# Two-layer FNet and attention kernel: single-row start, identity transposes, fused Newton steps, halved last copies

## The chip, the cores and the metric

One NeuronCore of a Trainium2 chip runs the kernel; the other cores are idle. The metric is the device time of one execution in microseconds (us). TensorE (PE in the profile, PEld for its weight loads) multiplies, VectorE (DVE), ScalarE (ACT) and GpSimd (POOL) compute elementwise, and SyncE (SP) issues most DMAs.

## What is computed

The input `x` is 2048 x 512, float32. Two layers run one after the other, each with the same weights:

```python
x = x + fnet(layernorm(x))       # Real(DFT_seq(DFT_hidden(.))): Cr @ (x @ Dr.T) - Ci @ (x @ Di.T)
x = x + attention(layernorm(x))  # 32 heads of 16; one k and one v shared by all heads; softmax; @ wo
...
def _layernorm(x, axis=-1, eps=1e-5):
    m = jnp.mean(x, axis=axis, keepdims=True)
    v = jnp.var(x, axis=axis, keepdims=True)
    return (x - m) / jnp.sqrt(v + eps)
```

## The kernel before

The sequence is cut into 16 row tiles of 128 (`NT`). Large products are made from two parts of each operand in a reduced format: a high part (`xnh`, `ch`) and the rest (`xnl`, `cl`). `mm3` (L86) issues three matmuls for one product: high by high, high by low, low by high. The low part is what is left after the high part is subtracted.

The order of work is written out by hand: every engine takes its instructions in the order of the code, and semaphores hold an instruction until what it needs is there. In phase A of a layer, `phase_a` loops over 128 steps `n`. In step `n` the matrix row tile `n % 16` of the sequence DFT is multiplied with the normalized row tile of the same number, into four accumulators `z`. The first 16 steps of layer 0 are those in which the rows are normalized, one after the other, two steps ahead of TensorE.

What the first steps do on each engine:

- `ld` and `c_load` issue the loads on SyncE: rows singly (256 KB), matrix tiles in pairs (`craw`, 512 KB, three buffers).
- `ln_stats` (L143, L144) takes mean and variance of a row on VectorE. `ln_root` (L149) takes the square root on ScalarE, for two rows, and adds `eps` to the variance on GpSimd (L150). `ln_inv` takes the reciprocal on VectorE (L156), then refines it by one Newton step, four small instructions on GpSimd (L157 to L160), or on VectorE where it is told so.
- `ln_app` normalizes a row in place on VectorE (L191). `ln_split` casts it to `xnh` on ScalarE (L658) and subtracts to get `xnl` on GpSimd (L659).
- `c_split` casts `craw` to `ch` on ScalarE (L78) and subtracts to get `cl` on VectorE (L79).
- `ln_step(n)` orders these: split row `n + 2`; in even steps the inverse of rows `n + 4` and `n + 5`; normalize row `n + 3`; in even steps the statistics of rows `n + 6` and `n + 7` and their root. In steps 4, 6, 8 and 10 `qd_zero` issues two DMAs from GpSimd (L121) behind that.

`a_start` writes out what comes before step 0: rows 0 and 1 are normalized together by `ln_rstd`, each operation an instruction of its own on VectorE.

Phase A also makes keys, values, queries and the maxima of the scores. Its last rows 14 and 15 are normalized singly, with `ln_inv` on VectorE, and transposed by `tr` (L268). Phase B is the attention: scores (L980), exponential (L983), product with the values (L994). `pv` copies a finished accumulator in two halves into one tile (L997 on ScalarE, L998 on VectorE). `finish` handles the last half tile of the last layer: four transposes of the copy (L1065), products with `wo` for the first half of the heads (`o_mm(0)`, `o_mm(1)`), scaling (L1070, L1073), two transposes (L1079), the split into high and low, the last products, and `o_add`, which adds to `x` (L1056) and issues the store on SyncE (L1057).

Of the kernel before, what the change touches and what calls it, by code (L numbers as in the profile page):

```python
# [17 lines left out]
P = 128  # L18
# [4 lines left out]
NT = S // P  # L23
# [16 lines left out]
]  # L40
ROWS = 48
KEPT = [e for e in EARLY if e[0]]
QSLOT = (8, 0, 1, "h", "l", 8, 0, 1, "h", "l", 8, 0, 1, 8, 0, 1)
HALF = NPAIR // 2
# [3 lines left out]
def fnet_mqa_kernel(ctx: ExitStack, tc: tile.TileContext, x_in, ct, dt_, wq, wkv, wo, out):  # L48
# [12 lines left out]
    def half(k, dtype=F32):  # L61
        return sb.tile([P, D], dtype, name=f"row{k}")
# [23 lines left out]
    def mm3(ps_, ah, al, bh, bl, start, stop):  # L86
        nc.tensor.matmul(ps_, ah, bh, start=start, stop=False)  # L87
        nc.tensor.matmul(ps_, ah, bl, start=False, stop=False)  # L88
        nc.tensor.matmul(ps_, al, bh, start=False, stop=stop)  # L89
# [51 lines left out]
    def ln_stats(x, t):  # L141
        st = sb.tile([P, 2, 6], F32, name="bst", bufs=2)
        nc.vector.bn_stats(st[:, 0, :], x)  # L143
        nc.vector.bn_aggr(mv[:, t, :], st[:, 0, :])  # L144

    def ln_root(t0, n):
        v = sb.tile([P, 4], F32, name="lnv", bufs=2)[:, :n]
        w = sb.tile([P, 4], F32, name="lnw", bufs=2)[:, :n]
        nc.scalar.activation(w, mv[:, t0:t0 + n, 1], AF.Sqrt, bias=eps)  # L149
        nc.gpsimd.tensor_scalar(v, mv[:, t0:t0 + n, 1], EPS, None, op0=ALU.add)  # L150
        return t0, n, v, w

    def ln_inv(t0, n, v, w, eng=None):
        r = rs[:, t0:t0 + n]
        e = eng or nc.gpsimd
        nc.vector.reciprocal(r, w)  # L156
        e.tensor_mul(w, r, r)  # L157
        e.tensor_mul(w, w, v)
        e.tensor_scalar(w, w, -0.5, 1.5, op0=ALU.mult, op1=ALU.add)
        e.tensor_mul(r, r, w)  # L160
# [35 lines left out]
    def make_layer(L, src, mid, dst, last):  # L196
# [11 lines left out]
        def c_load(n):  # L208
            if n < 128 and n % 2 == 0:
                tb, c, s = where(n)  # L210
                r = raws[n // 2] = raw_tile()
                if n < 112:
                    nc.sync.dma_start(r, ct[c, tb, s // 2])
                else:
                    h, sp = divmod(n - 112, 8)
                    for j in range(2):
                        nc.sync.dma_start(r[:, j, :].rearrange("p (a t) -> p a t", a=2),
                                          ct[c, tb, sp + j][:, :, 256 * h:256 * h + 256])

        def c_split(n):  # L220
            if n < 128:
# [386 lines left out]
        def a_start():  # L608
            if L:
                c_load(0)  # L610
                c_load(2)
            if L == 0:
                xs = {}

                def ld(t):
                    xs[t] = half(t % 8)
                    nc.sync.dma_start(xs[t], src[t])

                ld(0)
                ld(1)  # L620
                c_load(0)
                ld(2)
                ld(3)
                c_load(2)
                ld(4)
                ld(5)
                c_load(4)
                ld(6)
                ld(7)
                st["xs"], st["ld"] = xs, ld  # L630
                ln_stats(xs[0], 0)
                ln_stats(xs[1], 1)
                ln_rstd(0, 2)
                ln_app(0)
                ln_split(0)
                c_split(0)
                ln_app(1)
                ln_split(1)
                for t in (2, 3):
                    ln_stats(xs[t], t)  # L640
                r = ln_root(2, 2)
                c_split(1)
                for t in (4, 5):
                    ln_stats(xs[t], t)
                ln_inv(*r)
                st["root"] = ln_root(4, 2)
                ln_app(2)
            else:
                c_load(4)
                c_split(0)  # L650
                c_split(1)

        def ln_app(t):
            ln_apply(st["xs"][t], st["xs"][t], t)

        def ln_split(t):
            x = st["xs"][t]
            nc.scalar.copy(xnh[:, t, :], x)  # L658
            nc.gpsimd.tensor_sub(xnl[:, t, :], x, f(xnh[:, t, :]))  # L659

        def ln_step(n):
            if n + 2 < NT:
                ln_split(n + 2)
            if n % 2 == 0 and n + 4 < NT:
                ln_inv(*st["root"])
            if n % 2 == 0 and n + 8 < NT:
                st["ld"](n + 8)
                st["ld"](n + 9)
            if n + 3 < NT:
                ln_app(n + 3)  # L670
            if n % 2 == 0 and n + 6 < NT:
# [61 lines left out]
        def phase_a(extra):  # L733
# [120 lines left out]
            for n in range(128):  # L854
# [32 lines left out]
                                      lambda d: z_split_half(z[4 * h:4 * h + 4], h, d))  # L887
                for d in range(NK):
                    dsl = slice(d * P, (d + 1) * P)
                    if n < ROWS:  # L890
# [96 lines left out]
        def pv(i, s_):  # L987
            hf, c = divmod(s_, NT)
            if c == 0:
                acc[i, hf] = bank("z")  # L990
            a = acc[i, hf]
            pt = ptiles.pop((i, s_))
            for j in range(4):
                nc.tensor.matmul(a[32 * j:32 * j + 32, :], v1[:, c, :], pt[:, j, :], start=c == 0, stop=c == NT - 1)  # L994
            if c == NT - 1:
                oa = half(hf)
                nc.scalar.copy(oa[:, :256], a[:, :256])  # L997
                nc.vector.tensor_copy(oa[:, 256:], a[:, 256:])  # L998
                acc[i, hf] = oa

        bt = {}

# [38 lines left out]
            nc.gpsimd.tensor_copy(bt["oh"][:, cs], bt["ot"][:, cs])  # L1041
            nc.gpsimd.tensor_sub(bt["ol"][:, cs], bt["ot"][:, cs], f(bt["oh"][:, cs]))

        def o_mm(k):
            if k == 0:
                bt["po"] = bank("y")
            ks = slice(k * P, (k + 1) * P)
            mm3(bt["po"], bt["oh"][:, ks], bt["ol"][:, ks], woh[:, k, :], wol[:, k, :], k == 0, k == NK - 1)

        def o_proj(i):  # L1050
# [2 lines left out]
            o_add(i)  # L1053

        def o_add(i):
            nc.vector.tensor_add(bt["x"], bt["po"], bt["x"])  # L1056
            (nc.sync if last else nc.gpsimd).dma_start(dst[i], bt["x"])  # L1057

        def finish():
            i = NT - 1  # L1060
            oa = acc.pop((i, 1))
            x_load(i)
            pt = bank("y")
            for b in range(4):
                nc.tensor.transpose(pt[:, b * P:(b + 1) * P], oa[:, b * P:(b + 1) * P], ident)  # L1065
# [12 lines left out]
            for jj in range(2):  # L1078
                nc.tensor.transpose(pt[:, jj * P:(jj + 1) * P], on[:, jj * P:(jj + 1) * P], ident)  # L1079
# [176 lines left out]
```

## Time and profile before

| what | value |
|---|---|
| median of 3 runs | 3546.07 us (3544.29 to 3546.45) |
| profiled execution | 3549.72 us, span 3547.9 us |
| granted TensorE clock, mean | 0.995 |
| busy share of the span | PE 99%, DVE 77%, ACT 71%, POOL 23% |
| TensorE, 0 to 20 us | 10.11 us busy |
| TensorE, 20 to 40 us | 19.33 us busy |
| TensorE, 40 to 61.5 us | 20.47 us busy |

A row of a timeline gives the start in us, the duration in us, the engine, the line, the operation, what it writes and reads, the shapes, and in brackets the idle time of the engine before it with what ended it. A row of the waits gives the sum in us, the times and the longest. The difference between the profiled execution's time and its span lies around the program and is not touched by the change.

### The profile page before, as it was taken

Reading aid. Unit: us, or ns where it says so; the run is one execution under the profiler, and the core shown is the slowest. Engines: PE = TensorE matmul, PEld = TensorE weight load, DVE = VectorE, ACT = ScalarE, POOL = GpSimd, SP = SyncE. Lnnn points to the kernel's source line nnn. Section 1 sums busy time; section 2 is a strip of 40 time slices with the busy share of each in tenths; the row PEclk is TensorE's granted clock in tenths of the full one; section 3 lists DMA queues with packets and bytes.
Section 4 is the critical chain, followed back from the end, with each engine's and each line's share of the span. In section 5 each row is a group of like instructions: output and inputs, shape, how many; then the busy total and the mean of one; then the engine's idle time right before and its main releaser. Section 6 shows DMA issues by size and latency. Waiting matters only on the chain.

```text
span 3547.9 us, 64282 instructions
## 1 busy us (share of the span) xinstructions
PE 3505.9 (99%) x24576; PEld 1874.8 (53%) x24576; DVE 2714.7 (77%) x4892; ACT 2503.3 (71%) x3210; POOL 830.5 (23%) x1262
## 2 busy tenths in 40 slices
PE   8999999999999999999999999999999999999999
PEld 6887878433333333333378878883333333333333
DVE  6267776888888888888432777768888888888883
ACT  4223733888888888888932247438888888888888
POOL 4244342211221122112213443422101110111011
PEclk9999999999999999999999999999999999999999
DMA  6435252311111100111144342523111111011100
GB/s 191 150 144 167 80 165 87 85 56 34 35 35 51 36 23 23 49 34 26 40 137 128 127 150 90 153 66 88 47 37 35 49 34 38 23 35 37 37 23 25
DMA packets 224900, 254.55 MB, mean 72 GB/s; under 512 B 52880, under 2 KB 174800, under 8 KB 217424
## 3 DMA queue, kind: packets, MB, share of 16 engines
q1 hardware_dynamic: 210384, 233.12, 21.6%
q0 software_dynamic: 14208, 17.33, 1.6%
q8 instruction: 193, 3.16, 0.4%
q14 instruction: 115, 0.94, 0.1%
HBM read 187.16 MB, written 65.27 MB: 71 GB/s over the span
## 4 chain that ended last, share of the span: by engine, by line
PE 91%; issue 2%; DVE 2%; ACT 2%; POOL 1%; DMA 1%; SPq 0%; ACTq 0%; POOLq 0%; DVEq 0%
PE z L994 29%; PE x L980 19%; PE y L408 13%; PE x L809 11%; PE y L87 3%; PE y L88 3%; PE y L89 2%; PE y L475 2%; PE x L87 2%; PE x L89 2%; PE x L88 2%; PE x L593 1%; PE z L475 1%; DVE row L191 1%; POOL cl L79 1%
## 5 line engine op out<-in xcount | busy, mean ns | idle before, releaser
L983 ACT ACTIVATE slot<-x 128x1024 f32<-128x1024 f32 x2000 | 1945.9, 1024 | 284.5 <-PE x L980 276.2
L409 DVE TENSOR_REDUCE mxp<-y 128x1 f32<-128x512 f32 x2944 | 1849.6, 684 | 181.5 <-PE y L408 168.7
L994 PE MATMUL z<-slot,v 128*32 128x512 f32 x8192 | 1096.3, 605 | 1.6 <-DVE lnv L1105 0.7
L980 PE MATMUL x<-slot,kz 64*128 64x512 f32 x2976 | 677.3, 450 | 2.2 <-DMA slot<-craw 1.7
L980 PEld LDWEIGHTS x<-slot,kz 64*128 64x128 f32 x2976 | 279.2, 184 | 744.7 <-ACT slot L983 685.8
L408 PE MATMUL y<-kz,slot 64*128 64x512 f32 x2176 | 581.6, 397 | 1.9 <-DVE mxp L409 1.9
L809 PE MATMUL x<-cl,xnh 64*128 64x512 f32 (+1 forms) x1536 | 355.8, 357 | 0.0
L994 PEld LDWEIGHTS z<-slot,v 128*32 128x32 f32 x8192 | 163.4, 108 | 363.7 <-issue 332.8
L809 PE MATMUL x<-ch,xnh 64*128 64x512 f32 (+1 forms) x1536 | 348.1, 361 | 2.3 <-ACT row L796 2.2
L809 PE MATMUL x<-ch,xnl 64*128 64x512 f32 (+1 forms) x1536 | 346.2, 362 | 0.9 <-ACT xnl L580 0.9
L408 PEld LDWEIGHTS y<-kz,slot 64*128 64x128 f32 x2176 | 276.7, 186 | 22.8 <-DVE mxp L409 10.8
L79 POOL TENSOR_TENSOR cl<-craw,ch 128x512 fp32r<-128x512 f32 x176 | 223.9, 1295 | 225.5 <-ACT ch L78 174.3
L78 ACT CAST ch<-craw 128x512 fp32r<-128x512 f32 x256 | 154.6, 622 | 170.9 <-PE x L89 87.1
L475 PE MATMUL y<-kz,slot 64*128 64x512 f32 x690 | 271.7, 405 | 2.1 <-ACT rel L479 1.2
L543 POOL DMA_DIRECT2D slot<-mt x224 | 112.1, 508 | 585.2 <-PE y L408 490.1
L809 PEld LDWEIGHTS x<-ch,xnh 64*128 64x128 f32 x1536 | 213.1, 188 | 23.3 <-issue 5.2
L809 PEld LDWEIGHTS x<-cl,xnh 64*128 64x128 f32 x1536 | 217.7, 188 | 12.6
L489 DVE TENSOR_REDUCE mxe<-y 128x1 f32<-128x512 f32 x316 | 198.8, 679 | 29.3 <-PE y L475 28.7
L809 PEld LDWEIGHTS x<-ch,xnl 64*128 64x128 f32 x1536 | 209.7, 187 | 21.1 <-issue 5.9
L1035 POOL TENSOR_TENSOR row<-row,row 128x256 f32<-128x256 f32 x63 | 46.5, 738 | 700.3 <-DMA row<-rd 654.0
L87 PE MATMUL x<-ch,xnh 128*128 128x512 f32 x384 | 154.3, 402 | 9.1 <-ACT ch L78 8.4
L89 PE MATMUL x<-ch,xnl 128*128 128x512 f32 x384 | 153.4, 399 | 2.6 <-POOL xnl L659 2.6
(198 smaller groups left out, 4143.3 us busy)
## 6 DMA issues: line engine op xcount, KB each, us to landing
craw<-ct_in SPq DMA_DIRECT2D x112, 512.0 KB
slot<-qd SPq DMA_DIRECT2D x44, 1024.0 KB
qd<-row SPq DMA_DIRECT2D x144, 128.0 KB
od<-row SPq DMA_DIRECT2D x252, 64.0 KB
row<-wqd SPq DMA_DIRECT2D x48, 256.0 KB
row<-x_in SPq DMA_DIRECT2D x32, 256.0 KB
mid<-row POOLq DMA_DIRECT2D x32, 256.0 KB, 2.4
craw<-ct_in SPq DMA_DIRECT2D x32, 256.0 KB
```

Source lines behind the costliest of these rows:

```text
L79: (eng or nc.vector).tensor_sub(lo, raw, f(hi))
L87: nc.tensor.matmul(ps_, ah, bh, start=start, stop=False)
L88: nc.tensor.matmul(ps_, ah, bl, start=False, stop=False)
L89: nc.tensor.matmul(ps_, al, bh, start=False, stop=stop)
L408: nc.tensor.matmul(pm, o.qT[i][gs, pr, :], kz[gs, c0:c0 + n], start=True, stop=True)
L409: nc.vector.reduce_max(to, pm, axis=AX.X)
L475: nc.tensor.matmul(pm, o.qT[i][gs, pr, :], k[gs, c0:c0 + 512], start=True, stop=True)
L489: nc.vector.reduce_max(to, pm, axis=AX.X)
L809: nc.tensor.matmul(z[d], a[gs, s, d * P:(d + 1) * P], b[gs, :], start=first and q < 2 and e == 0, stop=last and q > 1 and e == len(turns) - 1)
L980: nc.tensor.matmul(st["e"][:, g, :], kz[64 * g:64 * g + KR, c * P:(c + 1) * P], o.qT[i][64 * g:64 * g + KR, cp:cp + 4, :], start=True, sto ...
L983: nc.scalar.activation(ptiles[i, s_][:, 2 * w:2 * w + 2, :], st.pop("e"), AF.Exp, scale=DH ** -0.5)
L994: nc.tensor.matmul(a[32 * j:32 * j + 32, :], v1[:, c, :], pt[:, j, :], start=c == 0, stop=c == NT - 1)
```

## The change

Six edits, at both ends of the kernel:

- Eleven transposes of the identity (`WARM`) are issued on TensorE ahead of the first matmul, into a buffer that nothing reads.
- Rows 0 and 1 are normalized one at a time (`first`): the normalized row is written straight to `xnh` by VectorE (a second L191-like instruction normalizes the row in place for `xnl`), and the matrix tile is split by `c_hi` and `c_lo`. The order of the instructions up to step 0 is changed with it. `c_split` skips tiles that are split already.
- The first matrix tile is loaded in two halves, each behind a row.
- In steps 0 and 1 of layer 0 TensorE does four matmuls of each kind (high by high, high by low, low by high) in turn, in place of three for each accumulator.
- `ln_inv` with an engine given uses three fused instructions (`scalar_tensor_tensor`); `ln_step` now gives it VectorE. Without an engine it does the former steps on GpSimd, and the addition of `eps` moves to it from `ln_root`.
- At the end, the second half of the last accumulator is copied to a tile of its own; one of the matmuls of `o_mm(1)` is moved behind the last transposes; the last addition and store are done in halves, the second store issued by ScalarE.

```diff
+WARM = 11
...
     def ln_root(t0, n):
-        v = sb.tile([P, 4], F32, name="lnv", bufs=2)[:, :n]
         w = sb.tile([P, 4], F32, name="lnw", bufs=2)[:, :n]
         nc.scalar.activation(w, mv[:, t0:t0 + n, 1], AF.Sqrt, bias=eps)
-        nc.gpsimd.tensor_scalar(v, mv[:, t0:t0 + n, 1], EPS, None, op0=ALU.add)
-        return t0, n, v, w
-
-    def ln_inv(t0, n, v, w, eng=None):
+        return t0, n, w
+
+    def ln_inv(t0, n, w, eng=None):
         r = rs[:, t0:t0 + n]
-        e = eng or nc.gpsimd
         nc.vector.reciprocal(r, w)
+        if eng:
+            eng.scalar_tensor_tensor(w, r, -0.5, r, op0=ALU.mult, op1=ALU.mult)
+            eng.scalar_tensor_tensor(w, mv[:, t0:t0 + n, 1], EPS, w, op0=ALU.add, op1=ALU.mult)
+            eng.scalar_tensor_tensor(r, w, 1.5, r, op0=ALU.add, op1=ALU.mult)
+            return
+        v = sb.tile([P, 4], F32, name="lnv", bufs=2)[:, :n]
+        e = nc.gpsimd
+        e.tensor_scalar(v, mv[:, t0:t0 + n, 1], EPS, None, op0=ALU.add)
...
+                def c_row(j):
+                    nc.sync.dma_start(raws[0][:, j, :], ct[0, 0, 0][:, j, :])
+
+                def c_hi(n):
+                    hls[n] = hl_tiles()
+                    nc.scalar.copy(hls[n][0], raws[n // 2][:, n % 2, :])
+
+                def c_lo(n):
+                    nc.vector.tensor_sub(hls[n][1], raws[n // 2][:, n % 2, :], f(hls[n][0]))
+
+                def first(t, r):
+                    ln_inv(*r, nc.vector)
+                    ln_apply(xnh[:, t, :], xs[t], t)
+                    c_lo(t)
+                    ln_app(t)
+                    nc.gpsimd.tensor_sub(xnl[:, t, :], xs[t], f(xnh[:, t, :]))
+
                 ld(0)
+                c_load(0)
+                c_row(0)
                 ld(1)
-                c_load(0)
+                c_row(1)
...
+                warm = bank("y")
+                for k in range(WARM):
+                    nc.tensor.transpose(warm[:, P * (k % 4):P * (k % 4) + P], ident, ident)
                 ln_stats(xs[0], 0)
+                r = ln_root(0, 1)
+                c_hi(0)
+                c_hi(1)
+                first(0, r)
                 ln_stats(xs[1], 1)
-                ln_rstd(0, 2)
-                ln_app(0)
-                ln_split(0)
-                c_split(0)
-                ln_app(1)
-                ln_split(1)
-                for t in (2, 3):
-                    ln_stats(xs[t], t)
+                r = ln_root(1, 1)
+                ln_stats(xs[2], 2)
+                first(1, r)
+                ln_stats(xs[3], 3)
                 r = ln_root(2, 2)
-                c_split(1)
+                c_hi(2)
+                c_lo(2)
+                ln_inv(*r, nc.vector)
+                ln_app(2)
                 for t in (4, 5):
                     ln_stats(xs[t], t)
-                ln_inv(*r)
                 st["root"] = ln_root(4, 2)
-                ln_app(2)
...
             if n % 2 == 0 and n + 4 < NT:
-                ln_inv(*st["root"])
+                ln_inv(*st["root"], nc.vector)
...
+                    if n < 2 and L == 0:
+                        for e in range(NK) if d < 3 else ():
+                            a, b = ((xnh, ch), (xnh, cl), (xnl, ch))[d]
+                            nc.tensor.matmul(z[e], a[:, s, e * P:(e + 1) * P], b, start=(n, d) == (0, 0), stop=False)
...
+                ob = half(0)[:, 256:] if last and (i, hf) == (NT - 1, 1) else oa[:, 256:]
                 nc.scalar.copy(oa[:, :256], a[:, :256])
-                nc.vector.tensor_copy(oa[:, 256:], a[:, 256:])
+                nc.vector.tensor_copy(ob, a[:, 256:])
...
+            if part:
+                for a, b in ((("oh", woh), ("oh", wol)), (("ol", woh),))[part - 1]:
+                    nc.tensor.matmul(bt["po"], bt[a][:, ks], b[:, k, :], start=False, stop=False)
+                return
...
+            if last and i == NT - 1:
+                for q, h in ((nc.sync, slice(0, 256)), (nc.scalar, slice(256, 512))):
+                    x = half(3)[:, h] if h.start else bt["x"][:, h]
+                    nc.vector.tensor_add(x, bt["po"][:, h], bt["x"][:, h])
+                    q.dma_start(dst[i][:, h], x)
+                return
...
-            o_mm(1)
+            o_mm(1, 1)
...
+            o_mm(1, 2)
```

More of the change, by code (lines that the diff above doesn't have):

```diff
@@ L211, in c_load @@
                 r = raws[n // 2] = raw_tile()
+                if n == L == 0:
+                    return
                 if n < 112:
@@ L220, in c_split @@
         def c_split(n):
-            if n < 128:
+            if n < 128 and n not in hls:
                 hls[n] = hl_tiles()
@@ L889, in phase_a @@
                     dsl = slice(d * P, (d + 1) * P)
-                    if n < ROWS:
+                    if n < 2 and L == 0:
+                        for e in range(NK) if d < 3 else ():
+                            a, b = ((xnh, ch), (xnh, cl), (xnl, ch))[d]
+                            nc.tensor.matmul(z[e], a[:, s, e * P:(e + 1) * P], b, start=(n, d) == (0, 0), stop=False)
+                        spend(pe=0.693)
+                    elif n < ROWS:
                         mm3(z[d], xnh[:, s, dsl], xnl[:, s, dsl], ch, cl, s == 0, s == NT - 1)
@@ L996, in pv @@
                 oa = half(hf)
+                ob = half(0)[:, 256:] if last and (i, hf) == (NT - 1, 1) else oa[:, 256:]
                 nc.scalar.copy(oa[:, :256], a[:, :256])
-                nc.vector.tensor_copy(oa[:, 256:], a[:, 256:])
-                acc[i, hf] = oa
+                nc.vector.tensor_copy(ob, a[:, 256:])
+                acc[i, hf] = (oa, ob) if last and (i, hf) == (NT - 1, 1) else oa
         bt = {}
@@ L1042, in o_hi, with o_mm @@
             nc.gpsimd.tensor_sub(bt["ol"][:, cs], bt["ot"][:, cs], f(bt["oh"][:, cs]))
-        def o_mm(k):
+        def o_mm(k, part=0):
             if k == 0:
@@ L1055, in o_add @@
         def o_add(i):
+            if last and i == NT - 1:
[3 more added lines that the diff above has]
+                    q.dma_start(dst[i][:, h], x)
+                return
             nc.vector.tensor_add(bt["x"], bt["po"], bt["x"])
@@ L1064, in finish @@
             for b in range(4):
-                nc.tensor.transpose(pt[:, b * P:(b + 1) * P], oa[:, b * P:(b + 1) * P], ident)
+                nc.tensor.transpose(pt[:, b * P:(b + 1) * P], oa[b // 2][:, (b % 2) * P:(b % 2 + 1) * P], ident)
             o_mm(0)
-            o_mm(1)
+            o_mm(1, 1)
             p4 = pt.rearrange("p (b j r) -> p b j r", b=4, j=4)
```

## The prediction

> **What bounds the kernel now.** I read the page first, then what TensorE waited for in the first 60 us, then the timeline of the first 60 us and of the last 10 us, then the places where VectorE and GpSimd stand in each other's way.
>
> ```profile
> span 3547.9 us, 64282 instructions
> PE 3505.9 (99%) x24576; PEld 1874.8 (53%) x24576; DVE 2714.7 (77%) x4892; ACT 2503.3 (71%) x3210; POOL 830.5 (23%) x1262
> ...
> PE x L87 <- ACT ch L78: 8.4, 1, 8.4
> PE x L89 <- POOL xnl L659: 2.6, 6, 0.9
> ```
>
> TensorE is busy 99% of the span, and what it loses before row 16 of the first stage is 8.4 us ahead of its first matmul and 2.6 us in six waits for the low part `xnl`. What it loses there nothing behind gives back, so the change is worth as much as the end of row 15 moves, plus the tail. But the rows come out of a loop over VectorE, ScalarE and GpSimd, and that loop must be read before TensorE's waits are. One pair of rows (steps 4 and 5):
>
> ```profile
> 26.95 1.53 DVE L191 TENSOR_SCALAR row<-row,mv,rs 128x512 f32<-128x512 f32 x1
> 28.41 0.68 DVE L79 TENSOR_TENSOR cl<-craw,ch 128x512 fp32r<-128x512 f32 x1
> 28.52 0.62 ACT L658 CAST xnh<-row 128x512 fp32r<-128x512 f32 x1 [1.17 <-DVE row L191]
> 29.01 0.15 DVE L156 RECIPROCAL rs<-lnw 128x2 f32<-128x2 f32 x1
> 29.08 0.52 DVE L191 TENSOR_SCALAR row<-row,mv,rs 128x512 f32<-128x512 f32 x1
> 29.22 1.54 POOL L659 TENSOR_TENSOR xnl<-row,xnh 128x512 fp32r<-128x512 f32 x1 [1.01 <-ACT xnh L658]
> 29.53 0.68 DVE L143 BATCH_NORM_STATS2 bst<-row 128x6 f32<-128x512 f32 x1
> 31.04 0.18 DVE L144 BATCH_NORM_AGGREGATE mv<-bst 128x2 f32<-128x6 f32 x1
> 31.52 0.60 ACT L78 CAST ch<-craw 128x512 fp32r<-128x512 f32 x1
> 31.98 1.24 POOL L121 DMA_DIRECT2D qd<-kz  x2
> 32.15 0.69 DVE L79 TENSOR_TENSOR cl<-craw,ch 128x512 fp32r<-128x512 f32 x1 [0.93 <-ACT ch L78]
> 32.76 2.07 DVE L191 TENSOR_SCALAR row<-row,mv,rs 128x512 f32<-128x512 f32 x1
> 33.24 1.30 POOL L659 TENSOR_TENSOR xnl<-row,xnh 128x512 fp32r<-128x512 f32 x1
> ...
> 3543.03 0.39 PE L87 MATMUL y<-slot,slot 128*128 128x512 f32 x1
> 3543.26 0.39 PE L88 MATMUL y<-slot,slot 128*128 128x512 f32 x1
> ```
>
> VectorE runs through it in order: normalize an even row (L191), `cl` (L79), reciprocal, normalize the odd row, statistics of two rows (29.53 to 31.22), then 0.93 us idle, because `ch` stands behind the square root (L149) on ScalarE, `cl`, and the next even row. From L191 of one even row to the next it is 32.76 - 26.95 = 5.81 us; ends taken, 34.83 - 28.48 = 6.35. TensorE needs 24 matmuls of 0.23 us (3543.03 to 3543.26) for the same two rows, 5.5 to 5.6 us. So VectorE's loop is already the slower one, and any instruction added to it between L191 and L191 is paid for in full. The four Newton steps and the addition of `eps` are on GpSimd today, outside it.
>
> The loop also shows who blocks whom. L191 takes 0.52 at 29.08, but 1.53 at 26.95 while GpSimd subtracts, and 2.07 at 32.76, where it starts in GpSimd's DMA issue (31.98 to 33.22), lets the subtraction behind it (33.24 to 34.54) pass too, and ends 0.29 after that. L79 at 32.15, inside the same DMA issue, is not slowed. Very small operations are held as well:
>
> ```profile
> 617.51 0.73 POOL L376 TENSOR_TENSOR row<-row,row 128x256 fp32r<-128x256 f32 x1 [1.16 <-ACT row L374]
> 617.85 0.41 DVE L157 TENSOR_TENSOR lnw<-rs 128x1 f32<-128x1 f32 x1
> 618.47 0.16 DVE L158 TENSOR_TENSOR lnw<-lnw,lnv 128x1 f32<-128x1 f32 x1 [0.21 <-POOL lnv L150]
> 619.05 0.88 DVE L191 TENSOR_SCALAR row<-row,mv,rs 128x512 f32<-128x512 f32 x1
> 620.08 0.63 PE L268 MATMUL z<-ident,row 128*128 128x128 f32 x4 [0.68 <-DVE row L191]
> ...
> 1728.90 0.73 POOL L1042 TENSOR_TENSOR slot<-row,slot 128x256 fp32r<-128x256 f32 x1
> 1728.93 0.72 DVE L532 TENSOR_TENSOR ms<-nm,ms 128x16 fp32r<-128x16 f32 x1
> ```
>
> A one-element product (L157) ends 0.02 after GpSimd's subtraction, at 618.26, where the next one (L158) takes 0.16, and a 16-column difference (L532) lasts 0.72, to 1729.65, again 0.02 behind. The statistics at 29.53 take their 0.68 beside the subtraction and are not held.
>
> **The change part by part: the start.**
>
> ```profile
> 3.46 0.69 DVE L143 BATCH_NORM_STATS2 bst<-row 128x6 f32<-128x512 f32 x1 [1.27 <-DMA row<-x_in]
> 5.84 0.16 DVE L182 TENSOR_TENSOR lnw<-rs 128x2 f32<-128x2 f32 x1
> 6.03 0.16 DVE L183 TENSOR_TENSOR lnw<-lnw,lnv 128x2 f32<-128x2 f32 x1
> 8.40 0.80 PE L87 MATMUL x<-ch,xnh 128*128 128x512 f32 x1 [8.40 <-ACT ch L78]
> 13.36 0.63 PE L87 MATMUL x<-ch,xnh 128*128 128x512 f32 x1
> 13.79 0.63 PE L88 MATMUL x<-cl,xnh 128*128 128x512 f32 x1
> 17.58 0.50 PE L87 MATMUL x<-ch,xnh 128*128 128x512 f32 x1
> ```
>
> Row 0 alone: statistics 3.46 to 4.36, root to 4.75, reciprocal, three small steps at 0.19 apart (5.84 to 6.03), L191 straight into `xnh`: 5.55 to 6.1. The first half of the matrix tile, now issued second, lands about where row 1 did, since the bytes ahead of it are the same, so `ch` is ready. First matmul about 6.15 instead of 8.40. The eleven transposes run between 1.3 and some 4 us on an idle engine and cost nothing. The extra loads cost SyncE one issue of some 0.4 us ahead of rows 2 to 7, which are needed 1 us or more after they land: nothing.
>
> Then VectorE: `cl` 0 and the second normalization of row 0 to 7.15, two statistics (0.8 each) to 8.8, inverse of row 1 and its two L191 and `cl` to 11.1, statistics of row 3 to 11.95, root, `ch` 2, `cl` 2 to 13.6, inverse of rows 2 and 3, row 2 normalized at 14.8, some 2 us earlier than today. But a new wait stands there: the cast of `xnh` 2 is queued on ScalarE behind the root of rows 4 and 5, and that waits for two statistics on VectorE, to 16.45. The cast runs from 16.75 to 17.35, and TensorE starts row 2 at 17.4 instead of 17.58. Of 2.25 us won, 0.2 are left, and TensorE stands idle for about 3 us ahead of it.
>
> **The loop.** Counted from E, the end of an even row's L191 (28.48): today the reciprocal runs at E+0.53, GpSimd's subtraction starts at E+0.74 and the odd row's L191 at E+0.60, ahead of it. With the three fused steps in between, the first comes up at E+0.72, in a dead heat with the subtraction, and of the three at least two, each with two inputs in SBUF, come after it. They are held to E+0.74+1.30 = E+2.05; the last ends near E+2.4. The odd row's L191 starts at about E+2.3 instead of E+0.60, and behind it on VectorE are both statistics, hence the root, `ch`, `cl` and the next even row. That adds 1.6 us to a pair without a DMA issue on GpSimd (5.81 to 7.4). In steps 4, 6, 8 and 10 the two DMAs of L121 now follow the subtraction at once (nothing is left between them on GpSimd) and hold the odd row's L191 for 1.05 to 1.24 more, to E+3.2; in exchange the next subtraction is no longer behind the DMAs, and the even row's L191 takes 1.53 again, not 2.07. A pair of these goes from 6.35 to about 8.4, +2.1.
>
> Fused steps have no row of their own in this trace. From below: they pass like L182, 0.19 each, 0.6 a pair and no hold. From above: held as L157 and L532 were. I take the hold, since these two are the same kind of operand at the same size. The Trainium skill (SBUF — State Buffer, the rules on the engine ports) says that a VectorE operation with two SBUF inputs and a GpSimd operation that reads SBUF take a shared port pair in turn, the loser waiting for the whole instruction. By that rule the fused steps are held too and the loop pays 1.6 to 2.1 a pair, where a rule for `tensor_tensor` alone would make it 0.6; the trace agrees for `tensor_tensor` (0.41 and 0.72 above), and no run here shows the fused form.
>
> Sum at the start: the pair of step 0 is held too (its third small step from 17.45 to 18.75), so row 4 is 1.3 late; +1.6 for step 2, 3 x 2.1 for steps 4, 6, 8 gives 9.2 at row 12; steps 10 and later have no statistics and add about 0.4. Row 15 ends **9.6** us later. For the clock see below: 0 to 2.3 more, I take 0.7. Start: **+10.3**.
>
> **Elsewhere.** The inverse of row 15 of each layer uses the fused form: no GpSimd addition to wait for (618.47) and one step less, so L191 starts at 618.7 and, if it is ahead of the subtraction that makes it 0.88 long at 619.05, ends near 619.25 instead of 619.93. TensorE waited 0.68 for it (620.08): 0.65 in each of two layers, **-1.3** (0 to -1.4). In the other places GpSimd does the addition just before its products instead of earlier: the same work in the same queue, nothing.
>
> ```profile
> 3538.76 0.37 ACT L997 COPY row<-z 128x256 f32<-128x256 f32 x1 [1.15 <-PE z L994]
> 3539.16 0.42 DVE L998 COPY row<-z 128x256 f32<-128x256 f32 x1 [24.50 <-ACT row L997]
> 3541.31 0.38 PE L1079 MATMUL y<-ident,row 128*128 128x128 f32 x2
> 3543.93 0.69 DVE L1056 TENSOR_TENSOR row<-y,row 128x512 f32<-128x512 f32 x1 [1.29 <-PE y L89]
> 3544.64 0.34 SPq L1057 DMA_DIRECT2D out_dram<-row  x1
> ```
>
> Tail: with a tile of its own the second copy starts 0.4 earlier, and one matmul of 0.23 leaves the way of the transposes at L1079, so the last matmuls end 0.35 earlier. Two half additions take 0.77 instead of 0.69 together, and the last transfer is half as long, which I put at 0.3 (0 to 0.4, since no row shows a transfer from ScalarE's queue; if that queue starts later than SyncE's, up to 0.5 the other way). **-0.65** (+0.1 to -1.0).
>
> Sum: 10.3 - 1.3 - 0.65 = **+8.4** on the profiled 3549.72, that is 3558.1; the median of the runs is 3.65 below it, so I forecast **3554.5**. A difference of 0.2% is 7.1 us, about what a measurement of this kernel can tell from none.
>
> **The rivals.**
>
> *The hold does not apply to the fused steps* (the statistics at 29.53 pass beside GpSimd, so a free form exists). Then a pair costs 0.6 more, less 0.5 where the DMAs move out of the way of the even row, and the late row 2 and 3 remain: +4 at the start, 3546.07 + 4 - 1.95 = 3548. *Only the DMA issue does not hold the odd row* (it slips in between the subtraction and the DMAs): 3 x 1 less, 3551.5.
>
> *Faster: TensorE, not VectorE's loop, is the bound.* For: TensorE 99% busy. Then 2.25 at the first matmul, the cold matmuls of row 0 (0.43 apart, 13.36 to 13.79, against 0.23: 12 x 0.2 = 2.4), the 2.6 of waits for `xnl` and 1.95 elsewhere are won: -9.2, 3536.9. It decides itself at one point: L191 of even rows must come at most 5.6 apart. Against: they are 5.81 apart today, with less work.
>
> *The clock.* TensorE's granted clock falls after a stretch with little work (columns: stretch; PE, PEld, DVE, ACT, POOL busy; granted clock; DMA share; GB/s):
>
> ```profile
> 280.70:284.10 3.40, 1.20 (x12) 0.62 (x10) 3.40 (x3) 0.01 (x1) 2.29 (x2) 1.00 0.67 236
> 284.20:287.50 3.30, 3.30 (x18) 2.57 (x18) 2.62 (x5) 1.96 (x4) 2.06 (x2) 0.50 0.47 144
> ```
>
> 1.20 us busy of 3.40, then 0.50 of the clock for 3.3 us. A pair of 8.4 with 5.6 of matmuls leaves gaps of nearly 3 us, so this can happen several times; most of it falls into waiting, but in rows 12 to 15 it costs 1.7 each. If it comes every pair: +4 more, 3558.5. The Trainium skill (TensorE: Matmul & The Clock Gate, PE-mode transpose) says that transposes don't count as work for the gate; by that the eleven would not open it, which changes the time here by nothing, because row 2 sets the pace either way.
>
> **How the numbers follow.** Hold with the DMA issues 0.62 (3552 to 3557, of which a sixth stays under 7.1), only the hold 0.14 (3551.5), no hold 0.13 (3548), clock every pair 0.06 (3558.5), faster 0.05. Slower by over 0.2%: 0.52 + 0.06 and a little from the second case, 0.61. Faster: 0.05. Within: 0.34. Range 3547.5 to 3559: it leaves out the faster case and a part of the ends.
>
> **What would show it.** Right: first matmul near 6.2 and row 2 near 17.4; fused steps of over 1 us beside L659; L191 of even rows 7.4 to 8.4 apart; L659's wait in front of TensorE larger than 2.6 us; row 16 some 10 us later than today. Wrong: fused steps all near 0.16, or even rows under 6 us apart.

## The result and the profile after

| | before | changed |
|---|---|---|
| median | 3547.39 us (22 runs, 3544.29 to 3550.55) | 3552.62 us (22 runs, 3549.3 to 3560.61) |
| profiled execution, span | 3549.72 us, 3547.9 us | 3553.05 us, 3551.3 us |
| row 2 starts on TensorE | 17.6 us | 18.5 us |
| row 12 | 49.3 us | 56.3 us |
| row 16 | 61.2 us | 67.5 us |

The ratio is 1.0016 (95% interval 1.001 to 1.0022): slower, by 3.5 to 7.8 us. The value itself lies below the 0.2% (7.1 us) on which the prediction put its chances (0.61 for slower by more than that, 0.34 for within), but the interval reaches past it, so it doesn't decide between the two. The forecast was 3554.5. The sign and the hold of the fused steps come out as forecast; several terms of the sum do not.

The page of the changed kernel, and what TensorE waited for in its first 72 us:

```profile
span 3551.3 us, 64294 instructions
...
PE 3508.0 (99%) x24587; PEld 1883.2 (53%) x24587; DVE 2721.4 (77%) x4914; ACT 2501.6 (70%) x3209; POOL 822.0 (23%) x1223
```

```profile
PE x L88 <- ACT xnh L689: 5.1, 5, 2.8
PE x L924 <- ACT ch L632: 3.6, 1, 3.6
PE x L90 <- POOL xnl L690: 3.5, 6, 0.6
```

The page still says 99%. The waits say more: the first matmul waits 3.6 us after the transposes, and a new wait of 5.1 us in five pieces has come up, for the cast `xnh`, the product of VectorE's loop. (The list names `ch` for the first wait. Row 0's own `ch` is through at 6.54 and its `xnh` at 7.40; the `ch` that ends at 7.42 is row 1's. In the kernel with the inverse back on GpSimd, below, row 1's `ch` ends at 7.70, after the first matmul at 7.52, and the list names `xnh`. So it is `xnh` that is waited for.) Here is that loop in the changed kernel, one pair of rows in its timeline (L197 is L191 of before, L80 was L79, L690 was L659, L122 was L121):

```profile
37.96 1.51 DVE L197 TENSOR_SCALAR row<-row,mv,rs 128x512 f32<-128x512 f32 x1
39.40 0.68 DVE L80 TENSOR_TENSOR cl<-craw,ch 128x512 fp32r<-128x512 f32 x1
40.00 0.15 DVE L154 RECIPROCAL rs<-lnw 128x2 f32<-128x2 f32 x1
40.18 0.16 DVE L156 SCALAR_TENSOR_TENSOR lnw<-rs 128x2 f32<-128x2 f32 x1
40.21 1.29 POOL L690 TENSOR_TENSOR xnl<-row,xnh 128x512 fp32r<-128x512 f32 x1 [1.02 <-ACT xnh L689]
40.38 1.14 DVE L157 SCALAR_TENSOR_TENSOR lnw<-mv,lnw 128x2 f32<-128x2 f32 x1
41.45 1.01 POOL L122 DMA_DIRECT2D qd<-kz  x2
41.55 0.16 DVE L158 SCALAR_TENSOR_TENSOR rs<-lnw,rs 128x2 f32<-128x2 f32 x1
41.63 0.57 DVE L197 TENSOR_SCALAR row<-row,mv,rs 128x512 f32<-128x512 f32 x1
...
45.29 1.52 DVE L197 TENSOR_SCALAR row<-row,mv,rs 128x512 f32<-128x512 f32 x1
```

The first fused step (L156) starts 0.03 us before GpSimd's subtraction (40.21) and takes its 0.16. The second (L157) lasts 1.14 us instead of 0.16 and ends 0.02 after the subtraction. Behind it stand the third step, the odd row, the statistics, the root, `ch`, `cl` and the next even row, which starts 45.29 - 37.96 = 7.33 us after the last. TensorE's matmuls for two rows take 5.6.

What starts the loop late stands in the timeline of the first 19 us:

```profile
4.44 1.28 ACT L149 ACT_TABLE_LOAD   x1 [4.44 <-DVE mv L145]
5.74 0.29 ACT L149 ACTIVATE lnw<-mv,eps 128x1 f32<-128x1 f32 x1
7.54 2.05 PE L924 MATMUL x<-ch,xnh 128*128 128x512 f32 x4 [3.59 <-ACT ch L632]
15.42 0.55 DVE L197 TENSOR_SCALAR row<-row,mv,rs 128x512 f32<-128x512 f32 x1
17.61 0.30 ACT L149 ACTIVATE lnw<-mv,eps 128x2 f32<-128x2 f32 x1 [3.61 <-DVE mv L145]
17.81 0.60 ACT L689 CAST xnh<-row 128x512 fp32r<-128x512 f32 x1
18.46 0.51 PE L88 MATMUL x<-ch,xnh 128*128 128x512 f32 x1 [2.78 <-ACT xnh L689]
```

The first root carries a load of ScalarE's function table, 1.28 us, which in the kernel before ran at 0.72, long before anything needed it. And row 2 is normalized by 15.97, but its cast stands behind a root that waits for two statistics: TensorE is idle for 2.78 us.

The tail, from the first copy of the last accumulator:

```profile
3542.63 0.37 ACT L1034 COPY row<-z 128x256 f32<-128x256 f32 x1 [1.15 <-PE z L1030]
3543.03 0.42 DVE L1035 COPY row<-z 128x256 f32<-128x256 f32 x1 [24.44 <-ACT row L1034]
...
3544.95 0.38 PE L1126 MATMUL y<-ident,row 128*128 128x128 f32 x2
...
3548.01 0.34 SPq L1101 DMA_DIRECT2D out_dram<-row  x1
3548.35 0.38 ACTq L1101 DMA_DIRECT2D out_dram<-row  x1
```

The second copy still waits for the first (`<-ACT row L1034`) although it now has a tile of its own. From the start of the first copy to the end of the execution it is 8.64 us, before it was 9.19.

### The profile page after: what moved, and what is told of

It reads as the page before. It is cut to its first block, busy times and chain, and to the rows that moved or that the text cites. A ratio compares the mean times of both kernels' runs of the same rounds, so it can differ in the third digit from the quotient of the medians.

```text
span 3551.3 us, 64294 instructions
## 1 busy us (share of the span) xinstructions
PE 3508.0 (99%) x24587; PEld 1883.2 (53%) x24587; DVE 2721.4 (77%) x4914; ACT 2501.6 (70%) x3209; POOL 822.0 (23%) x1223
## 4 chain that ended last, share of the span: by engine, by line
PE 90%; issue 3%; DVE 3%; ACT 2%; POOL 1%; DMA 0%; SPq 0%; ACTq 0%; DVEq 0%; POOLq 0%
PE z L1030 29%; PE x L1016 19%; PE y L416 13%; PE x L840 11%; PE y L88 3%; PE y L89 3%; PE y L90 2%; PE y L483 2%; PE x L88 2%; PE x L90 2%; PE x L89 2%; PE z L483 1%; DVE row L197 1%; ACT row L827 0%; PE y L1009 0%
## 5 line engine op out<-in xcount | busy, mean ns | idle before, releaser
L416 PEld LDWEIGHTS y<-kz,slot 64*128 64x128 f32 x2176 | 276.7, 186 | 22.9 <-DVE mxp L417 10.6
L80 POOL TENSOR_TENSOR cl<-craw,ch 128x512 fp32r<-128x512 f32 x176 | 225.9, 1304 | 222.7 <-ACT ch L79 159.8
L79 ACT CAST ch<-craw 128x512 fp32r<-128x512 f32 x253 | 152.7, 622 | 167.8 <-PE x L90 85.4
L840 PEld LDWEIGHTS x<-ch,xnl 64*128 64x128 f32 x1536 | 212.6, 187 | 18.6 <-issue 6.1
```

The source lines that it names most:

```text
L80: (eng or nc.vector).tensor_sub(lo, raw, f(hi))
L416: nc.tensor.matmul(pm, o.qT[i][gs, pr, :], kz[gs, c0:c0 + n], start=True, stop=True)
L840: nc.tensor.matmul(z[d], a[gs, s, d * P:(d + 1) * P], b[gs, :], start=first and q < 2 and e == 0, stop=last and q > 1 and e == len(turns) - 1)
```

## The experiments

Theory: the fused steps on VectorE, held by GpSimd's subtraction, lengthen the loop, and with it the start of row 16. Rivals: the late start alone (table load, cast behind the root), the DMA issue, TensorE's clock (for which the second profile of the changed kernel serves). The milestone is the start of row 16, which repeats to 0.1 us between profiles of one kernel (61.2 twice before, 67.5 twice changed); single times scatter by several us. "Apart" is from even row to even row on VectorE. The ratio is to the kernel before.

| run | row 2 | row 16 | apart | ratio | median |
|---|---|---|---|---|---|
| inverse on GpSimd | 18.4 | 61.9 | 5.80 to 6.34 | 0.9999 [0.999, 1.0008] | 3548.69 |
| inverse late | 18.2 | 59.6 | 5.68 to 5.70 | 0.9995 [0.9986, 1.0004] | 3545.89 |
| early table load | 17.2 | 66.3 | 7.3 | 1.0018 [1.0009, 1.0026] | 3553.45 |
| no transposes | 18.6 | 67.7 | 7.3 | 1.0012 [1.0003, 1.0021] | 3550.25 |
| tail and row 15 only | 17.6 | 61.5 | as before | 0.9998 [0.9989, 1.0006] | 3546.01 |
| cast first | 16.7 | 66.5 | 7.3 | 1.0011 [1.0002, 1.002] | 3551.57 |
| the three orders together | 15.5 | 57.9 | 5.68 to 5.71 | 0.9996 [0.9987, 1.0005] | 3546.48 |
| the same again | 15.4 | 57.8 | 5.67 to 5.70 | 0.9994 [0.9985, 1.0003] | 3546.66 |
| statistics spread | 15.4 | 62.2 | 6.86 to 7.07 | 1.0008 [0.9999, 1.0017] | 3549.92 |

**Inverse on GpSimd again**, all else as changed:

```diff
-                ln_inv(*st["root"], nc.vector)
+                ln_inv(*st["root"])
```

> The changed kernel, but the inverse of the row pairs in the first 16 steps is back on GpSimd (unfused, as before). Theory A (the three small steps on VectorE, one of them held by GpSimd's subtraction, set the pace): the L191 of even rows come 5.8 to 6.4 us apart instead of 7.3, row 16 starts on TensorE at about 62 instead of 67.5, and the time is 5 us below the changed kernel, about 1 us below the kernel before. Rival B (the late row 2, not the pace of the pairs, costs the time): the pairs stay near 7.3 and the time within 1.5 us of the changed kernel.

Row 16 comes 5.6 us earlier than in the changed kernel (61.9 against 67.5), though row 2 starts as late as there. So the steps on VectorE cost 5.6 of the 6.3 us, and the even rows are held beside the DMA issue as before:

```profile
33.23 2.07 DVE L197 TENSOR_SCALAR row<-row,mv,rs 128x512 f32<-128x512 f32 x1
33.70 1.30 POOL L690 TENSOR_TENSOR xnl<-row,xnh 128x512 fp32r<-128x512 f32 x1
```

**Inverse late:** the same fused steps on VectorE, behind the statistics instead of ahead of the odd row.

```diff
-            if n % 2 == 0 and n + 4 < NT:
-                ln_inv(*st["root"], nc.vector)
+            root = st["root"]
...
                 st["root"] = ln_root(n + 6, 2)
+            if n % 2 == 0 and n + 4 < NT:
+                ln_inv(*root, nc.vector)
```

> The changed kernel, but in even steps the inverse comes behind the two statistics and the root instead of ahead of the odd row; it stays on VectorE and fused. Theory A (what costs is the place, where the fused step meets the subtraction and stands ahead of the odd row): no fused step is held, the four small instructions fall into the 0.87 us in which VectorE waits for the cast of the matrix row, the pairs come 5.8 us apart, row 16 starts at about 61, the time is 6 us below the changed kernel. Rival (four more instructions on VectorE cost their 0.75 us wherever they stand): pairs 6.5 to 6.6 apart, row 16 at about 65.

Its timeline, between the statistics and the next even row:

```profile
30.24 1.24 POOL L122 DMA_DIRECT2D qd<-kz  x2
30.84 0.16 DVE L156 SCALAR_TENSOR_TENSOR lnw<-rs 128x2 f32<-128x2 f32 x1
31.03 0.16 DVE L157 SCALAR_TENSOR_TENSOR lnw<-mv,lnw 128x2 f32<-128x2 f32 x1
31.23 0.16 DVE L158 SCALAR_TENSOR_TENSOR rs<-lnw,rs 128x2 f32<-128x2 f32 x1
31.63 0.69 DVE L80 TENSOR_TENSOR cl<-craw,ch 128x512 fp32r<-128x512 f32 x1 [0.24 <-ACT ch L79]
32.24 1.55 DVE L197 TENSOR_SCALAR row<-row,mv,rs 128x512 f32<-128x512 f32 x1
```

Here all three steps fall into a DMA issue with no subtraction at work and take 0.16. They stand where VectorE waited for the root anyway (0.24 idle is left of 0.87), so they cost nothing, and row 16 comes 7.9 us earlier than in the changed kernel and 1.6 earlier than before. In the last pair, which has no statistics to stand behind, two steps are held: the first for 1.07 by a subtraction, the third for 2.06, until a DMA issue and the subtraction behind it are over.

```profile
45.90 1.49 POOL L690 TENSOR_TENSOR xnl<-row,xnh 128x512 fp32r<-128x512 f32 x1 [1.01 <-ACT xnh L689]
46.34 1.07 DVE L156 SCALAR_TENSOR_TENSOR lnw<-rs 128x2 f32<-128x2 f32 x1
...
47.64 2.06 DVE L158 SCALAR_TENSOR_TENSOR rs<-lnw,rs 128x2 f32<-128x2 f32 x1
```

It was the place of the steps, not their engine or number. A pair takes 7.33 us with the steps ahead of the odd row and 5.69 behind the statistics. Of these 1.6 us, 1.0 is the hold (1.14 against 0.16), and some 0.6 is what three steps at 0.19 apart take there even without it.

**Early table load:** a root of one column at the very start.

```diff
+    early = sb.tile([P, 1], F32, name="early")
+    nc.scalar.activation(early, ident[:, :1], AF.Sqrt)
```

> The changed kernel with one more instruction: a square root of one column of the identity on ScalarE, at its start. Theory A (the table load of ScalarE, which stood at 0.72 us in the kernel before, now stands at 4.44 behind the wait for the first statistics and delays every row by its 1.28 us): the load is back near 0.7, the first matmul comes at about 6.3 instead of 7.54, row 2 at about 17.3 instead of 18.46, row 16 1.2 us earlier, the time 1.2 us lower. Rival (the first rows have slack ahead of the slower pairs): first matmul earlier, row 16 where it was, time within 0.5 us.

```profile
0.72 1.28 ACT L102 ACT_TABLE_LOAD   x1 [0.72 <-PEq L1298]
2.02 0.20 ACT L102 ACTIVATE early<-ident 128x1 f32<-128x1 f32 x1
4.40 0.29 ACT L151 ACTIVATE lnw<-mv,eps 128x1 f32<-128x1 f32 x1 [2.18 <-DVE mv L147]
```

The first root runs at 4.40 instead of 5.74, the first matmul at 6.2 instead of 7.5, rows 2 and 16 come 1.2 earlier. That gain is smaller than what the times can show; the median isn't lower.

**No transposes** (`WARM = 0`):

> The changed kernel without the eleven transposes of the identity. Theory A (they are worth nothing, since row 2 sets the pace whatever the clock is): first matmul at 7.5, row 16 at 67.5, time within 0.7 us of the changed kernel. Rival (they open the clock sooner): the clock is granted in full up to 3.4 us later than 12.64, rows 0 and 1 end later, and the time rises by 1 us or more.

Row 0 starts at 7.7 and row 1 at 12.9, against 7.5 and 12.7 with the transposes: row 0 takes 5.2 us in both, 0.43 a matmul against 0.23 later. Two executions of one kernel differ by more than these two kernels do: in the second profile of the changed kernel row 0 takes 4.5. So the eleven transposes show no gain for the clock, and no cost; the times can't tell the two kernels apart. The Trainium skill (TensorE: Matmul & The Clock Gate, PE-mode transpose) states that a transpose doesn't count as work for the clock in the way a matmul does, and these two kernels agree with it. They don't prove it: TensorE also stands idle for 3.6 us between the transposes and the first matmul, and no run is without that gap.

**Tail and row 15 only:** the kernel before with the new `ln_inv` (its fused form is then used by rows 14 and 15 alone) and the edits of the end.

> The kernel before with the changed inverse function (so rows 14 and 15 of each layer use the fused steps on VectorE, rows of the first 16 steps stay on GpSimd) and the changed last copies, without any edit at the start. Theory A (these two parts are worth what was forecast for them, 1.3 and 0.65): row 16 starts at 61.2 as before, the transposes of row 15 come 0.7 earlier than those of row 14 allow today, the tail from the first last copy to the end is 0.5 to 0.6 shorter, the time 1.5 to 2 us lower. Rival (what follows row 15 waits for something else): row 16 the same, the tail 0.5 shorter, the time within 1 us of the kernel before.

Row 15's transposes follow those of row 14 after 4.81 us in both layers, before after 5.52; the last exponential to the end takes 12.02 instead of 12.50. Together -1.9, which fits the ratio but can't be told from no change by it.

**Cast first:** row 2 is split right after its normalization, ahead of the root of rows 4 and 5.

```diff
                 ln_app(2)
+                ln_split(2)
                 for t in (4, 5):
...
-            if n + 2 < NT:
+            if 0 < n < NT - 2:
                 ln_split(n + 2)
```

> The changed kernel, but the cast of row 2 stands ahead of the root of rows 4 and 5 on ScalarE instead of behind it. Theory A (the new wait behind the root delays row 2 by 1.7 us, and with it the first subtraction that holds a fused step): row 2 starts at about 16.7 instead of 18.46, no fused step is held in step 0, row 16 is 1 us earlier, the pairs stay 7.3 apart. Rival (row 2 has slack, the pairs set everything): row 2 at 16.7, row 16 at 67.5.

Row 2 starts 1.8 us earlier (16.7). The third step of step 0 now comes after the subtraction is over and takes 0.16 instead of 1.25, so row 4 is normalized 1.0 earlier (22.29 against 23.33), and so is row 16 on TensorE. The pairs stay 7.3 apart, as theory A had it; the other 0.8 turns into waiting.

**The three orders together** (inverse late, early table load, cast first), profiled twice:

> The changed kernel with three orders mended: table load early, cast of row 2 ahead of the root, inverse of the pairs behind the statistics. If the costs found are separate: first matmul at 6.2, row 2 at about 15.5, pairs 5.7 apart, row 16 at about 57.5 to 58.5, that is 3 us ahead of the kernel before; time about 4 to 5 us below it. If they overlap (the pairs catch the rest up): row 16 at 59.6 as with the late inverse alone, time 2 to 3 us below the kernel before.

> The kernel with the three orders mended, run again. Theory A (its start is 3.3 us ahead, and what moves single executions by up to 10 us is how many stretches of half clock TensorE falls into later): row 16 again at 57.9, even rows 5.7 apart; if this profile's time lies near 3548 instead of 3539, it shows 3 to 6 more stretches of 3.4 us at half clock behind row 16, each worth up to 1.7 us. Over the runs the median lies 2 to 5 us below the kernel before. Rival (the gain at the start is given back elsewhere, by a wait): the same number of half-clock stretches, and a stage that is longer by as much.

Row 16 at 57.9 and 57.8: 9.6 earlier than the changed kernel, 3.4 earlier than before. The even rows are 5.7 apart, close to the 5.6 that TensorE needs for two rows, so little is left to win in the loop. In time it lies clearly under the changed kernel but can't be told from the kernel before.

**Statistics spread:** the same, with the statistics of one row in each step, the inverse at the end of the even step and the root in the odd one.

> As the kernel with the three orders mended, and in the first 16 steps the statistics are spread, one row in each step, so that one of them runs on VectorE while GpSimd's subtraction would hold the next even row, and the cast of the matrix row no longer stands behind a root that waits for two statistics. If VectorE's loop is the bound: pairs at TensorE's own 5.6 us, TensorE without waits from row 3 on, row 16 at about 55 to 56.5, time 6 to 7 us below the kernel before. If something else bounds (loads, GpSimd): pairs stay at 5.7 and row 16 within 1 us of the kernel without the spreading.

Missed: 6.9 to 7.1 apart. The inverse came to stand beside a subtraction again, and its first step is held, in its timeline:

```profile
24.66 1.30 POOL L693 TENSOR_TENSOR xnl<-row,xnh 128x512 fp32r<-128x512 f32 x1 [1.02 <-ACT xnh L692]
24.83 1.15 DVE L158 SCALAR_TENSOR_TENSOR lnw<-rs 128x2 f32<-128x2 f32 x1
```

**Both kernels once more**, for how well a profile repeats:

> The changed kernel again, one look. Theory A: the start is the same to 0.3 us (row 2 at 18.5, row 16 at 67.5, fused steps held 1.15, odd row not held by the DMA issue), and the time differs from 3553.05 by 1.7 us for each half-clock stretch more or less. Rival (the start varies from execution to execution): row 16 off by 1 us or more.

> The kernel before again, one look. Theory A: row 16 at 61.2 to 61.5; time differs from 3549.72 with the number of half-clock stretches (8 runs of them with 10 windows in the first profile). Rival (the start varies): row 16 off by 1 us or more.

Row 16 at 67.5 and 61.2, as the first time; spans 3549.2 and 3547.8. In this second profile of the changed kernel the granted clock is at 0.50 from 17.8 to 24.6 us, twice as long as in the first, and row 16 starts at the same time, so the clock there does not set it.

**A product behind the DMA issue:** the changed kernel with one small GpSimd instruction more.

```diff
+    behind = sb.tile([P, 2], F32, name="behind")
...
             nc.gpsimd.dma_start(qd[t, rows, :], f(kz[:64 - M0, :]) if t < 4 else qd[0, rows, :])
+        if t < 4:
+            nc.gpsimd.tensor_mul(behind, ident[:, :2], ident[:, :2])
```

> The changed kernel with one more instruction: a product of two SBUF columns (128x2) on GpSimd, ready at any time and read by nothing, right behind the two DMA issues of steps 4, 6, 8 and 10. In the changed kernel the odd row's normalization starts 0.2 us into these issues and takes 0.54 to 0.57; in the kernel before, the even row's normalization at the same place takes 1.88 to 2.56, and there a subtraction with its cast done stands behind the issues. Theory A (what stands ready behind the issue claims the operands' way ahead of time and holds VectorE through the issue): the odd row's normalization, or a fused step just ahead of it, takes 1.0 to 1.4 in these steps, even rows come 7.8 to 8.2 apart instead of 7.3 in steps 4 to 10, and row 16 starts on TensorE at 69.0 to 70.5 instead of 67.5. Theory B (the issue never holds; in the kernel before it was the subtraction alone, which began while the normalization was still at work): the normalization stays at 0.54 to 0.6, the product costs at most 0.2, even rows 7.3 apart, row 16 at 67.4 to 67.9. The time moves by no more than the start does.

```profile
34.18 1.34 POOL L124 DMA_DIRECT2D qd<-kz  x2
34.37 0.54 DVE L201 TENSOR_SCALAR row<-row,mv,rs 128x512 f32<-128x512 f32 x1
35.55 0.21 POOL L126 TENSOR_TENSOR behind<-ident 128x2 f32<-128x2 f32 x1
```

The normalization stays at 0.54 to 0.57, rows 7.3 apart, row 16 at 67.6: theory A of this run has fallen. Theory B explains three of the four long normalizations of before, where the subtraction began while the normalization would still have been at work, but not the fourth:

```profile
50.79 1.06 POOL L121 DMA_DIRECT2D qd<-kz  x2
50.89 2.55 DVE L191 TENSOR_SCALAR row<-row,mv,rs 128x512 f32<-128x512 f32 x1 [0.92 <-POOL rs L160]
51.86 1.29 POOL L659 TENSOR_TENSOR xnl<-row,xnh 128x512 fp32r<-128x512 f32 x1
```

It would have been over at 51.41, 0.45 before the subtraction began, and yet took 2.55. The step held at 47.64 in the kernel with the late inverse is of this kind too: its subtraction began at 48.36. A subtraction of full size in place of the product was not tried. What holds VectorE there stays open.

## Why the prediction was right or wrong

**The hold: right.** The prediction has "at least two" of the fused steps come after the subtraction and wait for it. So the rows show it: one step is itself held, for 1.14 to 1.25 in each pair, and what is left of the three waits behind it. That the place beside the subtraction is the cause, the late inverse and the spread statistics show together. A pair without the DMA was forecast at 7.4 and takes 7.3. The Trainium skill (SBUF — State Buffer, Who interferes with whom) states that a VectorE instruction with two SBUF inputs contends with a GpSimd instruction that reads SBUF. The trace agrees for the fused form with an operand of 128x2: 1.14 us beside the subtraction against 0.16.

**The DMA term: wrong.** The step that failed is that the two DMAs of L121 "hold the odd row's L191 for 1.05 to 1.24 more". In the changed kernel that row starts 0.2 us into the issue and takes 0.54 to 0.57. The hold was taken over from the even row of the kernel before without knowing its condition. On VectorE it is 29.30 us from the normalization of row 4 (23.33) to that of row 12 (52.63), before it was 24.12 (21.14 to 45.26): 5.2 more, forecast 1.6 + 3 x 2.1 = 7.9, so 2.7 of the term was not there. This was the rival "only the DMA issue does not hold the odd row", with its chance of 0.14, whose 3551.5 lies 1.1 under the measured median.

**The start of the loop: forecast too early.** First matmul 7.54 instead of 6.15, row 2 at 18.46 instead of 17.4. The step that failed is "root to 4.75": the table load of 1.28 us had been out of sight because it ran beside other work, and nothing in the argument asked what it would stand behind. The early table load gives it back (6.2, 17.2). The cast behind the root was foreseen and is there.

**Clock: right in kind.** After the wait for row 2 the granted clock falls to 0.50 for one stretch (19.5 to 22.9 us; in the second profile for two), at a point where TensorE waits for rows anyway:

```profile
15.90:19.30 3.40, 0.74 (x2) 0.30 (x2) 2.87 (x9) 0.80 (x2) 0.81 (x1) 1.00 0.11 42
19.50:22.80 3.30, 2.98 (x7) 2.41 (x8) 2.36 (x7) 0.92 (x3) 0.26 (x1) 0.50 0.00 0
```

It does not come again in the loop, in which a pair leaves 1.7 us of gaps and not 3.

**The rows behind the loop.** The forecast added 0.4 from row 12 to row 15 and lost nothing there; in fact row 16 is 6.3 late where row 12 was 7.0 late. Row 14's normalization is the one that was held for 2.55 at 50.89 in the kernel before; in the changed kernel it starts at 57.40 and takes 0.54. The prediction did not name this gain.

**Row 15: half right.** In layer 0 the transposes come 0.71 earlier, forecast 0.65, with the fused step held for 0.40 as the small product was. In layer 1 of the profiled execution they come 0.75 later, in the second profile 0.63 later. The timeline and the list of DMA issues of that stretch show why:

```profile
2379.12 0.54 POOL L585 DMA_DIRECT2D mid<-row  x1 [4.83 <-DVE row L584]
...
2381.85 0.16 DVE L158 SCALAR_TENSOR_TENSOR rs<-lnw,rs 128x1 f32<-128x1 f32 x1
...
2383.50 0.55 DVE L197 TENSOR_SCALAR row<-row,mv,rs 128x512 f32<-128x512 f32 x1 [1.49 <-DMA mid<-row]
```

```profile
mid<-row POOLq DMA_DIRECT2D x1, 256.0 KB, 4.3
```

The row is normalized in place while its old value is still being stored to `mid`. The store landed after 4.3 us here; with the tail and row 15 only, it landed after 2.3 and hid:

```profile
mid<-row POOLq DMA_DIRECT2D x1, 256.0 KB, 2.3
```

So the gain of 0.65 is there when the store is quick, and a wait that the prediction had not named takes its place when it is not. Twelve profiles here are of kernels with the fused step in row 15. In layer 0 all of them have the gain (0.64 to 0.71); in layer 1 ten wait for the store, and only the kernel without transposes and the one with the tail and row 15 only don't. In those ten the transposes of row 15 come as late as before or up to 0.9 later. Why the store takes 2.3 or 4.3 isn't settled.

**Tail: right in sum, wrong in its parts.** Forecast -0.65, measured -0.55. The step "the second copy starts 0.4 earlier" failed: it waits for the first copy with a tile of its own too. Both read the same accumulator, which is the likely reason, but no run separates that. The moved matmul brought the last transposes 0.23 forward (2.32 behind the first copy, before 2.55); the other 0.3 lies behind the last matmul, where the addition and the store are halved.

**The sum.** 6.3 at the start, less 0.71 in layer 0, less 0.55 at the tail, and -0.71 to +0.75 in layer 1: 4.3 to 5.8. The ratio says 3.5 to 7.8. The forecast was +8.4, of which +10.3 at the start, 4.0 too high. There the DMA term was 2.7 too high, rows 12 to 16 1.1, the clock 0.7, and the late start of the loop, with the table load in it, 0.9 too low (row 4 came 2.2 late, forecast 1.3), together 3.6. The other 0.4 lies in where one reads: row 12 comes 7.4 late on VectorE but 7.0 on TensorE. Between the medians the change is +5.2. That the forecast time missed by only 1.9 is partly luck: the change itself was forecast 3.2 too high, with errors of both signs in it, and the 3 runs it started from lie 1.3 below the 22.

## What to carry to other kernels

An instruction moved to another engine is priced by what stands beside it there, and by everything queued behind it: three steps of 0.16 us cost 1.6 a pair ahead of the odd row (7.33 against 5.69), and nothing behind the statistics. Before putting a small operation with two inputs on VectorE, look in the timeline for GpSimd's elementwise instructions at that place, and put it into a gap that VectorE already has. A hold or a wait seen on one instruction should not be carried over to another before its condition is known, and a load or store that is hidden today should be listed with the spare time that hides it.

## What was not expected of the hardware

TensorE's granted clock can move the time of a single execution by more than the change does. It falls to 0.50 for stretches of 3.4 us, behind stretches of the same length with 0.74 (above), 1.20 (in the prediction) or 2.41 us of matmuls, and whether it falls differs between executions of one kernel. The two profiles of the kernel with the three orders, at the same place (columns: stretch; PE, PEld, DVE, ACT, POOL busy; granted clock; DMA share; GB/s):

```profile
295.30:298.70 3.40, 2.43 (x17) 1.28 (x14) 2.55 (x5) 1.13 (x4) 0.27 (x1) 1.00 0.00 0
298.80:302.10 3.30, 3.30 (x18) 2.43 (x18) 1.74 (x3) 0.53 (x1) 0.00 (x0) 1.00 0.00 0
```

```profile
295.30:298.70 3.40, 2.41 (x15) 1.29 (x13) 2.55 (x5) 1.21 (x4) 0.16 (x1) 1.00 0.00 0
298.80:302.10 3.30, 3.30 (x10) 2.54 (x9) 1.64 (x3) 0.00 (x0) 0.00 (x0) 0.50 0.00 0
```

With nearly the same work behind it (2.43 and 2.41 us busy), the second execution has 10 matmuls where the first has 18. The first profile has 6 such stretches of 3.4 us in all, the second 11; row 16 starts at 57.9 and 57.8 in both, and the spans are 3537.7 and 3546.7. That is 9.0 us for 5 stretches. Half the clock over 3.4 us can cost at most 1.7, so 8.5 of the 9.0 at the most. Over the 14 profiles, which have 6 to 11 such stretches behind row 16, what follows the start of row 16 lasts 3479 to 3489 us and is longer by some 1.3 for each of them (a straight line through them, correlation 0.89). The changed kernel's profile has 9, of which 8 behind row 16, the kernel before's 10, which is part of why the spans differ by only 3.4 us. Effects of 1 to 3 us are therefore read from a place in the timeline that repeats, such as the start of row 16, and not from a median of a dozen runs.
